# A hand-ordered FFT mixing kernel: output pair 0 in cosine and sine parts, and a re-ordered list of operations

## The chip, the cores and the metric

The kernel runs on one core of a Trainium2 chip. The core has five engines that work side by side: TensorE (PE in the profile, with weight loads as PEld), VectorE (DVE), ScalarE (ACT), GpSimd (POOL) and SyncE (SP), which here only issues transfers. Every engine takes its own instructions strictly in order and waits for the others by semaphores. The metric is the time of one launch in device microseconds (us), lower is better; the median of three runs of the kernel before is 114.5 us (114.27 to 114.72).

## What is computed

The input x is 2048 x 1024 (rows S, columns D, bfloat16). Two spectral filters A and B are applied to the same x, and a gate for each row mixes them:

```python
x = A_x
g = _sigmoid((x * gate_w).sum(-1, keepdims=True))
a = irfft2(rfft2(x) * (A_w_r + 1j * A_w_i)).astype(bfloat16)
b = irfft2(rfft2(x) * (B_w_r + 1j * B_w_i)).astype(bfloat16)
return g * a + (1 - g) * b
```

The two weights are 2048 x 513 complex each.

## The kernel before

The transforms are matrix products with small constant tables. The 2048 rows are split as 16 x 128 (s1, s2); the columns are folded by their symmetry into cosine and sine parts of even and odd frequencies. "Unit" n runs over 16 pieces of the spectrum: n = 0 to 7 hold the even column frequencies (par 0), n = 8 to 15 the odd ones (par 1). After the weights, the way back goes through a scratch tensor in device memory, which is written by unit and read by pair v: pair v holds output rows s1 = 2v and 2v+1, so there are 8 pairs of two rows (s = 0, 1), and each row has a first and a second half (h = 0, 1).

**The list.** The order of all work is written out by hand in the string ORDER (lines 24 to 65), some 570 tokens. A token names a function, its indices, then a PSUM bank (0 to 7) or an engine (A = ScalarE, D = VectorE, P = GpSimd, S = SyncE). Lines 856 to 858 call the functions in that order, and each engine runs its own tokens in the order of the list. Nothing reorders them later. So a token's place in the list decides what waits behind it on its engine, and a PSUM bank that is named again makes the later product wait until the earlier one has been read.

The stages, with their tokens and lines:

- **Forward along the rows.** x: (249) loads x in nine transfers. F1 (323 to 336) makes the even (e) or odd (o) part of one s1 on TensorE, 8 products of 128 columns. FC (411, copy on L201 or L203) moves half of it out of PSUM and FD (424, L422) folds both halves on VectorE, two operations of 256 elements; or FX (429) moves all of it and FP (435, also L422) folds on GpSimd. The result is the tile y. neg (275, L280) makes a negated table.
- **Forward along the columns, weights.** F2 (521, L528) and its copy T (532), F3 (549, L569) and its copy X (572), then the product with the weights P (577, L586), always on VectorE, 128 x 4096 elements. Y, NA and N (591 to 615) patch the two special columns of units 0 to 7: a small product on TensorE and two small operations on VectorE.
- **Back along the columns.** J (618, L632), 32 small products for each of the 16 units, needs P of its unit (and N, for units 0 to 7). R copies one half of it out of PSUM, on ScalarE (L201) or VectorE (L203). H (651, L654) stores that half to the scratch tensor and L:par:v (656, L665) loads pair v back, both on SyncE's queue: an L waits until all H of its par have landed.
- **The gate.** gc, GH, GC, Gt, GK, GZ, GS make sigmoid values from y; GA (L515) and GB (L519) make tables EA and EB of them on VectorE, four s1 at a time, with both inputs in SBUF. tab (299) runs a sigmoid once on ScalarE to load its table.
- **Back along the rows, and out.** V:par:v:s:bank (668, L675) applies EA and EB to one row of a pair, 8 products; VC (678) copies it to SBUF (two buffers). Then the last column transform: U (696, L703) makes a whole row in four products of 512 columns; C (705, L712) makes only the cosine part (256 columns) and the sine part (256 columns), in four products of 256. The two halves of the output row are cosine plus sine and cosine minus sine.

For par 0 the C result goes to EV, which holds the even part of a row: EX copies both parts to SBUF and EQ (803, L806) adds or subtracts them, on VectorE or GpSimd; or ES copies the sine part and EF (792, L796) does both sums on VectorE; or E (783) copies the two parts as they are, unsummed.

For par 1 the odd part is added to and subtracted from EV. Three ways are in use:

- OR (824, L826), two operations a row on VectorE, straight from a U in PSUM.
- OC (813) copies a U to SBUF and OP (819, L822) does the two operations on GpSimd.
- "Cosine and sine parts": EV was filled by E, unsummed, and the odd part is made by C. QD (828, L833) adds and subtracts par 1's parts to EV's parts on VectorE, two operations a row, into a float32 tile pq; then QP (835, L838) sums cosine and sine, four operations a pair (h, g), each over both rows, from pq in SBUF.

S:S:v (840, L847) stores a finished pair, in two halves for pair 7.

Of the kernel before, what the change touches and what calls it, by code (L numbers as in the profile page):

```python
# [29 lines left out]
FP:2:o FD:9:o FP:4:o F1:7:o:6 FX:6:o:A FD:8:e FD:9:e FC:10:e:A F1:13:e:5 c:S:PM FC:13:e:A F1:12:e:1 FC:12:e:A F1:5:o:4  # L30
FX:7:o:A F1:15:e:2 FC:15:e:A FD:11:e FD:10:e FD:12:e FD:13:e FX:5:o:A F1:13:o:7 F1:14:e:6 FP:6:o F1:15:o:0 FD:15:e FC:13:o:A
FP:7:o FP:5:o pw:P F1:12:o:4 FC:14:e:A F1:8:o:1 F1:10:o:5 FC:12:o:A FC:8:o:A FD:14:e FC:10:o:A neg:D:0:4 neg:D:4:16 FD:13:o
F2:1:1:2 F2:1:0:6 F2:0:0:3 FC:15:o:A T:1:1:A FD:10:o FD:8:o FD:12:o T:1:0:A W:S:2 W:S:6 T:0:0:A F1:14:o:7 F2:0:1:5 F1:11:o:6
T:0:1:A F3:1:2 FD:15:o FC:11:o:A F2:2:0:5 F2:2:1:4 FC:14:o:A X:1:A F3:0:0 FD:11:o T:2:0:A T:2:1:A X:0:A F2:4:1:6 F2:3:1:5
FD:14:o Y:1:4 T:3:1:A P:1:b F2:4:0:3 F2:3:0:2 Y:0:7 F3:2:0 GH:5 T:3:0:A T:4:0:A NA:1:D W:S:10 W:S:5 P:0:b W:S:3 W:S:7
c:S:WJ:4:16 F3:3:3 X:2:A W:S:9 NA:0:D T:4:1:A W:S:11 N:1:D W:S:4 GC:A J:1:6:0 F2:5:0:2 F2:5:1:5 P:2:b X:3:A R:1:1:A R:1:0:A
W:S:8 c:S:IG T:5:0:A Y:3:4 Y:2:1 Gt:0 F2:7:0:3 F3:4:6 T:5:1:A F2:7:1:2 X:4:A T:7:1:A N:0:D P:3:b GK:D NA:2:D NA:3:D N:2:D
J:0:0:4 N:3:D T:7:0:D R:0:1:A J:3:2:6 R:0:0:D GZ:0:0 F3:5:4 R:3:0:A R:3:1:D Y:4:6 GS:0 F2:6:0:7 X:5:A J:2:0:2 T:6:0:A P:4:b
NA:4:D R:2:0:D Y:5:4 R:2:1:A F2:6:1:7 GZ:1:5 T:6:1:A N:4:D GS:1 H:0:1 F3:7:1 H:1:0 H:3:0 H:0:0 H:1:1 X:7:A F2:8:1:5 T:8:1:A
# [872 lines left out]
```

## Time and profile before

| | |
|---|---|
| median of three runs | 114.5 us |
| the profiled execution's own time | 114.51 us |
| its span, first to last instruction | 112.7 us |
| mean granted TensorE clock | 0.987 |
| transfers | 36.79 MB, 326 GB/s over the span |
| HBM read, written | 23.96 MB, 12.58 MB |

The profile gives for each engine the time in which it was busy, the chain of work that ended last (followed back from the last instruction), groups of like instructions with their mean duration, and a timeline. Back-to-back operations of one engine overlap a little in the profile, so that eight operations of 0.68 us can take 4.87 us in a row: the step from one to the next (the pitch) is shorter than the duration. A number behind "x" is a count of instructions; in brackets or behind a bar stands the idle time before them, and what ended it.

### The profile page before, as it was taken

What the parts mean: (1) busy time and instruction counts of PE and PEld (TensorE: products, weight loads), DVE (VectorE), ACT (ScalarE), POOL (GpSimd) and SP (SyncE); (2) the same over time, 40 slices, a digit from 0 to 9 for tenths busy, and PEclk for the clock granted to TensorE, in tenths of its full rate; (3) what the DMA queues carried; (4) which work ended last, traced back from release to release, by engine and by line L of the source; (5) the groups of instructions that cost most, each with busy time, mean ns of one, the idle gap of its engine ahead of it and who ended that gap; (6) DMA issues with size and microseconds to landing.
All of it is one profiled execution on the core that took longest, in us unless ns stands there. A gap on an engine that the chain in (4) does not pass through costs nothing.

```text
span 112.7 us, 3824 instructions
## 1 busy us (share of the span) xinstructions
PE 99.4 (88%) x1556; PEld 69.8 (62%) x1559; DVE 100.1 (89%) x160; ACT 86.2 (76%) x141; POOL 43.0 (38%) x64
## 2 busy tenths in 40 slices
...
GB/s 70 368 309 398 405 379 400 398 260 413 410 412 412 372 298 326 394 298 186 237 302 292 420 407 307 385 377 325 295 246 398 337 385 329 196 192 186 372 372 186
DMA packets 17794, 36.79 MB, mean 326 GB/s; under 512 B 1904, under 2 KB 10736, under 8 KB 17776
## 3 DMA queue, kind: packets, MB, share of 16 engines
...
q8 instruction: 12, 0.20, 0.7%
...
HBM read 23.96 MB, written 12.58 MB: 324 GB/s over the span
## 4 chain that ended last, share of the span: by engine, by line
PE 32%; DVE 27%; DMA 16%; ACT 10%; issue 7%; SPq 4%; DVEq 1%; ACTq 0%
DVE p L586 9%; DVE y L422 9%; PE ps L703 8%; DMA ro<-sc 6%; DMA re<-in_x_dram 5%; DVE rl L203 5%; PE ps L632 5%; PE ps L528 5%; PE ps L675 5%; DMA sc<-rl 5%; ACT rl L201 4%; PE ps L569 4%; ACT T L201 3%; SPq L665 3%; PE ps L336 3%
## 5 line engine op out<-in xcount | busy, mean ns | idle before, releaser
L806 POOL TENSOR_TENSOR re<-wx 128x256 f32<-128x256 f32 x10 | 10.7, 1089 | 55.8 <-ACT wx L201 55.8
L201 ACT COPY wx<-ps 128x256 f32<-128x256 f32 (+1 forms) x41 | 18.3, 475 | 8.0 <-PE ps L336 4.5
L201 ACT CAST rl<-ps 128x1024 bf16<-128x1024 f32 x23 | 22.8, 1069 | 0.8 <-PE ps L632 0.6
L201 ACT CAST V<-ps 128x512 bf16<-128x512 f32 x26 | 14.9, 616 | 8.8 <-PE ps L675 4.4
L632 PE MATMUL ps<-p,wj 32*64 32x512 bf16 x512 | 18.2, 380 | 1.1 <-ACT rl L201 0.6
L528 PE MATMUL ps<-fd,y 128*128 128x256 bf16 x128 | 17.1, 273 | 1.3 <-ACT T L201 0.8
L586 DVE TENSOR_TENSOR p<-X,ro 128x4096 bf16<-128x4096 bf16 x8 | 18.2, 2278 | 0.0
L201 ACT CAST X<-ps 128x1024 bf16<-128x1024 f32 x16 | 17.3, 1079 | 0.1
L422 DVE TENSOR_TENSOR y<-ps,wx 128x256 bf16<-128x256 f32 x48 | 16.4, 414 | 0.5 <-ACT wx L201 0.5
L336 PE MATMUL ps<-f,re 128*128 128x128 bf16 x256 | 15.2, 219 | 1.6 <-DMA re<-in_x_dram 1.5
L336 PEld LDWEIGHTS <-re 128*128 128x128 bf16 x256 | 14.6, 98 | 2.4 <-DMA re<-in_x_dram 2.2
L201 ACT CAST T<-ps 128x512 bf16<-128x512 f32 x26 | 15.5, 647 | 0.5 <-PE ps L528 0.3
L528 PEld LDWEIGHTS <-y 128*128 128x128 bf16 x128 | 11.3, 97 | 5.9 <-issue 4.5
L632 PEld LDWEIGHTS <-wj 32*64 32x64 bf16 x512 | 8.3, 103 | 7.6 <-issue 4.1
L422 POOL TENSOR_TENSOR y<-wx 128x256 bf16<-128x256 f32 x16 | 11.3, 732 | 2.6 <-ACT wx L201 2.1
L826 DVE TENSOR_TENSOR ot<-re,ps 128x512 bf16<-128x512 f32 x18 | 11.3, 682 | 0.9 <-PE ps L703 0.4
L703 PE MATMUL ps<-ig,V 128*128 128x512 bf16 x45 | 11.2, 379 | 0.2
L712 PE MATMUL ps<-ig,V 128*128 128x256 bf16 x80 | 10.9, 273 | 0.2 <-ACT rl L201 0.2
L203 DVE CAST rl<-ps 128x1024 bf16<-128x1024 f32 x9 | 10.9, 1215 | 0.2 <-PE ps L632 0.2
L569 PE MATMUL ps<-T,wf 64*64 64x512 bf16 (+1 forms) x128 | 10.1, 333 | 1.1 <-DVE rl L203 0.4
L838 POOL TENSOR_TENSOR ot<-pq 128x512 bf16<-128x512 f32 x8 | 10.0, 1281 | 0.0
L675 PEld LDWEIGHTS <-re 128*128 128x128 bf16 x128 | 7.8, 98 | 2.4 <-issue 1.3
...
## 6 DMA issues: line engine op xcount, KB each, us to landing
sc<-rl SPq DMA_DIRECT2D x32, 256.0 KB, 4.1
...
```

The costliest lines, as they stand in the source:

```text
L201: nc.scalar.copy(out=out, in_=in_)
L203: Q[e].tensor_copy(out=out, in_=in_)
L336: nc.tensor.matmul(o, lhsT=lh, rhs=rh, start=(h == 0), stop=(h == 1))
L422: Q[e].tensor_tensor(yo[:, v, k:k + n, s1, :], a.rearrange("p (k c) -> p k c", c=4), b.rearrange("p (k c) -> p k c", c=4), op)
L528: nc.tensor.matmul(ps[:, v * 256:v * 256 + 256], lhsT=y[:, v, par, b, 2 * t:2 * t + 2, :, :].rearrange("p j s c -> p (j s c)"), rhs=C["FD" ...
L569: nc.tensor.matmul(view(ps[ho, tt * 512:(tt + 1) * 512], dst), lhsT=lh, rhs=view(T[hp(jh), tt, :], src), start=(w == 0), stop=(w == 1))
L586: nc.vector.tensor_tensor(p[:], xb, wb, ALU.mult)
L632: nc.tensor.matmul(o, lhsT=lh, rhs=src[r, ri, wi, tt], start=(q == 0), stop=(q == 3))
L675: nc.tensor.matmul(ps[:, ch * 128:ch * 128 + 128], lhsT=RR[par][:, v, ch // 2, s, c0 + 256 * ab:c0 + 256 * ab + 128], rhs=Ew[:, s1, :], st ...
L703: nc.tensor.matmul(ps, lhsT=Vs[par, v][:, s, ch, :], rhs=rh, start=(ch == 0), stop=(ch == 3))
L712: nc.tensor.matmul(ps[:, o:o + 256], lhsT=Vs[par, v][:, s, ch, :], rhs=g[:, o:o + 256], start=(ch % 2 == 0), stop=(ch % 2 == 1))
L826: nc.vector.tensor_tensor(otile(v)[:, s, h, :], EV[:, v, s], PS["O", 1, v, s], (ALU.add, ALU.subtract)[h])
```

## The change

Only the string ORDER changes; no function does. The list has 571 tokens in place of 572, and nearly all its lines differ, because tokens move by a few places and PSUM banks are renumbered.

**Pair 0.** Its even part is no longer summed: E:0:0 and E:0:1 on VectorE take the place of EX:0 (two, ScalarE) and of four EQ:0 (three on GpSimd, one on VectorE). Its odd part is made by C:1:0:0 and C:1:0:1 in place of two U; four QD:0 on VectorE and four QP:0 (three on GpSimd, QP:0:1:1 on VectorE) take the place of OC:0:0, two OP:0 (GpSimd) and two OR:0 (VectorE). Pairs 3 and 6 were already done in this way.

**Engines.** QP:3:1:1 and QP:6:1:0 move from GpSimd to VectorE. Of the EQ of pairs 1, 2 and 7, four move from VectorE to GpSimd and one (EQ:2:0:0) the other way. Of copies, VectorE gives up FX:1:o, one R and one T on balance, and takes some of VC, EX, ES and E in exchange for others. VectorE no longer has GB:12 close to the end of the weight products; it stands right after P:8.

**Order.** tab stands ahead of the first copy. The weight loads W and the constants are issued in another order. P keeps its order (1, 0, 2, 3, 4, 5, 7, 6, 8, 9, 10, 11, 12, 14, 13, 15). Behind the last scratch store, pairs of par 1 are loaded in the order 3, 1, 0, 5, 6, 7, 2, 4 (before 1, 3, 6, 7, 0, 2, 4, 5), and used by TensorE in the order 3, 1, 0, 6, 5, 2, 7, 4 (before 1, 3, 6, 0, 2, 5, 7, 4, by each pair's first V).

The start of the list, the lines around P:6 and P:8, and its end, before (-) and after (+):

```diff
-warm:8 c:A:F1 x:S:0:1 x:S:1:1 c:A:gws F1:0:o:4 x:S:2:2 F1:0:e:1 F1:1:e:6 F1:1:o:5 FC:0:e:A FC:1:e:A tab:A x:S:4:2 x:S:6:2
-c:S:E x:S:8:2 FX:0:o:D x:S:10:2 FD:0:e FD:1:e F1:2:e:7 F1:3:e:2 F1:3:o:0 FX:1:o:D FC:3:e:A F1:2:o:5 F1:5:e:4 x:S:12:2
...
-Y:7:0 F2:9:1:5 R:5:1:A F3:8:2 NA:7:D T:9:0:D F2:10:1:0 T:9:1:D F2:10:0:4 X:8:A T:10:1:A N:7:D GA:D:8 T:10:0:A F3:9:2 GA:D:4
-W:S:14 H:2:1 X:9:A J:7:6:0 N:6:D GA:D:0 P:8:b J:6:2:4 W:S:12 H:2:0 R:7:1:A H:3:1 R:6:0:D W:S:15 R:7:0:A H:5:0 H:5:1 GB:D:4
...
-V:0:2:0:2 VC:0:2:1:A VC:0:2:0:A EX:1:1:A H:12:0 J:14:0:4 J:13:6:2 R:14:0:A P:15:b H:11:1 R:14:1:A R:13:0:A C:0:2:1:1
-C:0:2:0:5 EX:2:0:A H:12:1 EX:2:1:D V:0:1:0:4 GB:D:12 R:13:1:D J:15:0:6 V:0:6:1:5 VC:0:1:0:A C:0:1:0:2 R:15:1:A V:0:6:0:4
-H:14:0 H:14:1 GB:D:8 R:15:0:D H:13:0 H:13:1 VC:0:6:1:A H:15:1 H:15:0 VC:0:6:0:A V:0:4:1:3 V:0:5:1:6 L:0:3 EX:1:0:A L:1:1
-L:1:3 L:1:6 EQ:0:0:1:D C:0:6:1:0 V:0:5:0:4 VC:0:5:1:D VC:0:5:0:D E:6:1:A EQ:2:1:0:D EQ:0:1:1:P L:1:7 L:1:0 L:1:2 L:1:4
-C:0:6:0:2 C:0:5:1:7 VC:0:4:1:A V:0:7:0:6 C:0:5:0:1 L:1:5 V:0:4:0:4 ES:5:1:A V:0:7:1:5 EQ:1:1:1:P VC:0:4:0:A E:6:0:D
-VC:0:7:0:D C:0:7:0:6 VC:0:7:1:A C:0:4:1:4 C:0:4:0:0 EX:7:0:A V:0:3:1:5 EQ:0:1:0:P EQ:2:0:1:P EQ:1:1:0:P EQ:2:0:0:P EQ:0:0:0:P
-EQ:2:1:1:P V:0:3:0:6 C:0:7:1:2 EQ:1:0:0:D VC:0:3:1:A VC:0:3:0:A EQ:1:0:1:D ES:5:0:D EF:5:1 EF:5:0 ES:4:1:D EF:4:1 C:0:3:1:5
-C:0:3:0:1 EX:7:1:A E:3:1:A E:3:0:A ES:4:0:A V:1:1:1:6 V:1:1:0:3 V:1:3:0:7 VC:1:1:0:A V:1:3:1:2 VC:1:3:0:A U:1:1:0:3
-VC:1:3:1:A EQ:7:0:0:D C:1:3:0:1 C:1:3:1:2 V:1:6:1:5 VC:1:1:1:D EF:4:0 EQ:7:1:1:D QD:3:0:0 OC:1:0:A QD:3:1:0 QD:3:1:1 QD:3:0:1
-U:1:1:1:3 EQ:7:0:1:P EQ:7:1:0:P OP:1:0:1 V:1:0:1:7 QP:3:0:1:P OP:1:0:0 QP:3:0:0:P VC:1:0:1:D VC:1:6:1:A C:1:6:1:5 V:1:0:0:6
-V:1:6:0:2 VC:1:0:0:A VC:1:6:0:A OR:1:1:1 U:1:0:1:7 QP:3:1:0:P U:1:0:0:1 QD:6:1:0 OR:1:1:0 OC:0:0:A V:1:2:1:4 VC:1:2:1:A
-OR:0:1:1 QD:6:1:1 QP:3:1:1:P C:1:6:0:0 V:1:2:0:2 V:1:5:1:5 V:1:5:0:4 OR:0:1:0 OP:0:0:1 QD:6:0:0 OP:0:0:0 QD:6:0:1 VC:1:2:0:D
-QP:6:1:0:P QP:6:0:1:P QP:6:1:1:P S:S:1 VC:1:5:1:A VC:1:5:0:A U:1:2:1:1 U:1:5:1:0 V:1:7:0:6 S:S:3 U:1:5:0:7 U:1:2:0:2
-V:1:7:1:5 V:1:4:0:4 VC:1:7:0:A V:1:4:1:3 OR:2:1:0 VC:1:7:1:A OR:2:1:1 OR:5:1:0 OR:5:1:1 OR:5:0:0 VC:1:4:0:A U:1:7:0:1
-OR:5:0:1 OR:2:0:0 S:S:0 QP:6:0:0:P VC:1:4:1:A U:1:4:0:4 S:S:5 OR:2:0:1 OR:7:0:1 OR:7:0:0 U:1:7:1:5 U:1:4:1:0 OC:4:0:A S:S:2
-OR:7:1:0 S:S:7:0 OR:7:1:1 S:S:6 OP:4:0:0 OP:4:0:1 OR:4:1:1 OR:4:1:0 S:S:7:1 S:S:4
+warm:8 c:A:F1 x:S:0:1 x:S:1:1 F1:0:o:0 F1:0:e:5 F1:1:e:3 F1:1:o:1 c:A:gws FX:0:o:D x:S:2:2 tab:A x:S:4:2 F1:2:e:2 x:S:6:2
+x:S:8:2 F1:3:e:6 FP:0:o gc:P FC:1:e:A c:S:E x:S:10:2 x:S:12:2 FX:1:o:A FC:0:e:A FD:1:e FC:2:e:A x:S:14:2 c:S:w0 FD:0:e
...
+R:5:0:A R:5:1:A T:9:0:A H:2:0 W:S:15 W:S:14 W:S:13 Y:7:4 T:9:1:D GA:D:4 F3:8:2 F2:10:1:1 F2:10:0:6 X:8:A T:10:0:A Y:6:0
+NA:7:D P:6:b H:4:0 H:4:1 NA:6:D F3:9:4 N:7:D N:6:D T:10:1:D J:7:6:0 P:8:b X:9:A R:7:1:A J:6:2:4 R:7:0:A GB:D:12 R:6:0:D
...
+R:12:1:A H:9:0 V:0:1:1:7 C:0:0:0:6 V:0:2:0:4 VC:0:1:1:A C:0:1:1:7 VC:0:2:1:A F3:15:2 VC:0:2:0:A R:12:0:D P:13:b EX:1:1:A
+J:14:0:4 H:10:1 H:9:1 X:15:A R:14:1:A H:10:0 H:11:0 H:12:1 E:0:0:D J:13:6:2 P:15:b R:14:0:A V:0:1:0:5 R:13:0:A H:12:0 H:11:1
+R:13:1:D C:0:2:1:4 J:15:0:6 VC:0:1:0:A EX:2:1:A R:15:0:A GB:D:8 R:15:1:D C:0:1:0:5 EX:1:0:A V:0:6:0:4 C:0:2:0:3 EQ:2:1:0:D
+V:0:6:1:1 VC:0:6:0:A V:0:5:1:0 H:14:1 V:0:5:0:5 EX:2:0:D H:14:0 H:13:1 H:13:0 C:0:6:0:7 VC:0:6:1:A VC:0:5:1:A H:15:0 E:6:0:A
+H:15:1 VC:0:5:0:A C:0:6:1:4 C:0:5:1:1 E:6:1:A L:0:3 EQ:2:0:0:D ES:5:1:D L:1:3 EQ:1:1:1:P EQ:1:1:0:P V:0:4:1:6 V:0:4:0:2
+V:0:7:1:5 C:0:5:0:3 EQ:2:1:1:P EQ:1:0:1:P VC:0:4:1:A EF:5:1 VC:0:4:0:D ES:5:0:D L:1:1 L:1:0 C:0:4:1:0 EQ:2:0:1:P EF:5:0
+C:0:4:0:7 V:0:7:0:6 VC:0:7:1:A C:0:7:1:4 V:0:3:1:5 VC:0:7:0:D V:0:3:0:1 C:0:7:0:3 ES:4:1:A ES:4:0:A EF:4:0 EX:7:1:D
+VC:0:3:1:A C:0:3:1:7 VC:0:3:0:A EX:7:0:A V:1:3:1:5 V:1:3:0:2 C:0:3:0:3 E:3:1:D L:1:5 L:1:6 L:1:7 L:1:2 VC:1:3:1:A VC:1:3:0:A
+EQ:1:0:0:P EQ:7:1:0:P C:1:3:1:7 EQ:7:0:1:P C:1:3:0:2 EF:4:1 E:3:0:A EQ:7:0:0:P QD:3:1:1 V:1:1:1:0 L:1:4 QD:3:0:1 VC:1:1:1:A
+V:1:1:0:1 V:1:0:0:6 U:1:1:1:0 VC:1:1:0:A VC:1:0:0:A V:1:0:1:3 C:1:0:0:6 QD:3:1:0 QD:3:0:0 U:1:1:0:5 VC:1:0:1:A V:1:6:1:2
+OC:1:0:A EQ:7:1:1:P QP:3:1:1:D C:1:0:1:3 VC:1:6:1:A OR:1:1:1 OR:1:1:0 V:1:5:0:1 V:1:6:0:5 V:1:5:1:2 QD:0:0:1 QD:0:0:0
+QD:0:1:1 C:1:6:1:6 QD:0:1:0 QP:0:1:1:D QD:6:1:0 QP:3:1:0:P QP:3:0:1:P QP:3:0:0:P VC:1:5:0:A VC:1:5:1:A VC:1:6:0:A S:S:3
+U:1:5:0:4 OP:1:0:1 V:1:2:1:1 C:1:6:0:7 U:1:5:1:2 V:1:2:0:3 QP:0:0:0:P QD:6:1:1 OP:1:0:0 V:1:7:0:5 VC:1:2:1:A U:1:2:1:6
+OR:5:0:1 V:1:7:1:0 QP:0:0:1:P VC:1:2:0:A OR:5:0:0 QP:0:1:0:P QD:6:0:0 S:S:1 VC:1:7:0:A U:1:2:0:1 OR:5:1:1 OR:5:1:0 QD:6:0:1
+OR:2:1:0 QP:6:0:0:P V:1:4:0:3 QP:6:1:1:P OR:2:1:1 VC:1:7:1:A VC:1:4:0:A U:1:7:0:0 V:1:4:1:2 S:S:5 S:S:0 U:1:4:0:6 U:1:7:1:5
+QP:6:0:1:P VC:1:4:1:A U:1:4:1:7 OR:2:0:0 OR:2:0:1 OR:7:0:1 OR:7:0:0 QP:6:1:0:D S:S:2 OR:7:1:1 S:S:7:0 OC:4:0:A OP:4:0:1 S:S:6
+OP:4:0:0 OR:7:1:0 S:S:7:1 OR:4:1:0 OR:4:1:1 S:S:4
```

More of the change, by code (lines that the diff above doesn't have):

```diff
@@ L30 @@
[L30 to L39, printed above, removed]
```

29 lines of the change are left out of this document (19 added, 10 removed).

## The prediction

> **What bounds the kernel now.** I read the page's busy shares first, then the stretches, the chain of waits, and the timelines of VectorE and GpSimd.
>
> ```profile
> span 112.7 us, 3824 instructions
> PE 99.4 (88%) x1556; PEld 69.8 (62%) x1559; DVE 100.1 (89%) x160; ACT 86.2 (76%) x141; POOL 43.0 (38%) x64
> 24.89:80.06 55.17, 50.50 (x964) 31.58 (x964) 54.90 (x59) 53.98 (x76) 8.14 (x7) 1.00 0.96 345
> 80.06:109.20 29.14, 26.84 (x284) 19.87 (x284) 26.12 (x50) 15.02 (x30) 19.84 (x18) 1.00 0.81 302
> 87.46:107.60 20.14, 19.44 (x191) 13.22 (x191) 17.43 (x31) 9.84 (x19) 16.59 (x14) 1.00 0.74 286
> ```
>
> Columns of the last three rows: the stretch, its length, then busy time of PE, PEld, DVE, ACT, POOL, the granted clock, transfers. From the first weight product (24.89) to the last scratch copy of VectorE (80.06), VectorE is busy 54.90 of 55.17 us and ScalarE 53.98. From 87.46 to 107.60 TensorE is busy 19.44 of 20.14. So there are two bounds in turn: VectorE, with ScalarE just beside it, and then TensorE, with VectorE close behind. A new wait on the bounding engine is paid in full, and only less work or fewer waits there can gain.
>
> ```profile
> 1.63 6.08 DMA re<-in_x_dram
> 10.61 8.88 DVE y L422 x26
> 79.00 1.15 DVE rl L203
> 80.16 2.38 DMA sc<-rl
> 85.72 7.16 DMA ro<-sc
> 92.92 0.62 PE ps L675 x8
> 96.60 0.45 PE ps L675 x8
> 97.05 0.44 PE ps L712 x4
> 104.06 3.47 PE ps L703 x16
> 107.56 0.41 DVE ot L826
> 108.57 0.60 DVE ot L826
> ```
>
> These pieces of the chain (start, length, what) show the joints: the third x transfer lands at 7.71; folds run from 10.61; the last copy R:15, its store, the loads of odd pairs; TensorE; two OR. They price TensorE: a V 0.45, a C 0.44, a U 3.47/4 = 0.87. VectorE ends at 109.17, and the last store takes the span to 112.7.
>
> **The front: 0 (from -0.6 to +0.5).**
>
> ```profile
> 20.25 4.71 DVE L422 TENSOR_TENSOR y<-ps,wx 128x256 bf16<-128x256 f32 x14
> 24.89 2.27 DVE L586 TENSOR_TENSOR p<-X,ro 128x4096 bf16<-128x4096 bf16 x1
> 6.22 1.28 ACT L301 ACT_TABLE_LOAD   x1
> L201 ACT COPY wx<-ps 128x512 f32<-128x512 f32 x16 | 10.0, 624 | 2.4 <-PE ps L703 2.3
> 10.29 0.33 SPq L254 DMA_DIRECT2D fd<-cst_fd  x1
> fd<-cst_fd SPq DMA_DIRECT2D x2, 256.0 KB, 6.2
> 19.71 1.47 PE L528 MATMUL ps<-fd,y 128*128 128x256 bf16 x12
> ```
>
> At 10.61 the 26 folds begin that run into the two negs and these 14, without a gap to 24.89. After the change the first five FD still wait for the third x transfer, which keeps its place in the queue, and FD:5 again starts near 10.6, with the same 40 folds and two negs behind it. The FX:1:o that VectorE gives up (about 0.6) is lost in that wait, as is the 1.28 us table load on ScalarE. Behind FC:14:e, X:1 now has one FX more ahead of it on ScalarE (0.5 in a row; that is the +0.5), but ScalarE, without the table load, is ahead by about as much there. The table FD:0:1 was issued at 10.29 and lands some 6.2 later, 16.5, for an F2 at 19.71; it is now queued behind WF:4:16 and PM, 0.5 MB more, which at the mean 326 GB/s is 1.6 us, and that fits.
>
> **The middle: the last R 0.5 earlier (from -0.8 to +1.0).**
>
> ```profile
> L203 DVE CAST rl<-ps 128x1024 bf16<-128x1024 f32 x9 | 10.9, 1215 | 0.2 <-PE ps L632 0.2
> L203 DVE CAST V<-ps 128x512 bf16<-128x512 f32 x6 | 4.1, 691 | 1.2 <-PE ps L675 1.1
> L203 DVE CAST T<-ps 128x512 bf16<-128x512 f32 x6 | 3.9, 681 | 0.0
> 54.07 0.41 DVE L519 TENSOR_TENSOR eb<-e,ea 128x512 bf16<-128x512 bf16 x1
> 76.37 0.94 DVE L519 TENSOR_TENSOR eb<-e,ea 128x512 bf16<-128x512 bf16 x1
> 74.07 2.27 POOL L806 TENSOR_TENSOR re<-wx 128x256 f32<-128x256 f32 x1 [3.26 <-ACT wx L201]
> L806 POOL TENSOR_TENSOR re<-wx x10: 719/731/2429, 68.4 to 87.5; 128x256 f32<-128x256 f32 x10
> 73.48 2.28 DVE L586 TENSOR_TENSOR p<-X,y 128x4096 bf16<-128x4096 bf16 x1
> ```
>
> In this stretch VectorE loses one T, one R and one EX (pitches of 0.60, 1.14, 0.61) and gains two VC and two E (four times 0.61): +0.1. ScalarE gains a T and an R and loses two VC and two EX: about -0.6, so it is no new bound. The other part is contention. The GB at 76.37 took 0.94, the one at 54.07 0.41; GpSimd was in an EQ in the first case and idle in the second. The other way round, the EQ that began at 74.07, inside P:15, took 2.27 where the median is 0.731. So an operation of either engine with both inputs in SBUF can hold the other up. After the change GB:12 stands behind P:8, with GpSimd idle: -0.5 (0 if GpSimd meets it anyway). One thing speaks against: J:7 needs N:7, now behind P:6, and a PSUM bank that T:10:0 frees behind a later X:8. It comes about 0.7 later and ScalarE slips with it; X:10 has more than that in hand before P:10, so 0 (0.7 if not). The last R then ends at 80.06 + 0.1 - 0.5 = 79.6.
>
> **The joint at J:15.** Behind P:15 (before: 73.48 to 75.76) VectorE now has only R:13:1, GB:8 and R:15:1, 1.14 + 0.4 + 1.14 = 2.7 us, where it had 4.3; E:0:0 stands ahead of P:15. So P:15 ends at 79.6 - 2.7 = 76.9, and
>
> ```profile
> 64.35 1.33 PE ps L632 x32
> 76.85 1.07 PE L632 MATMUL ps<-p,wj 32*64 32x512 bf16 x32
> 77.85 0.23 PE L675 MATMUL ps<-ea,re 128*128 128x128 bf16 x1
> ```
>
> J:15, 1.33 for its 32 products, ends near 78.3, where before TensorE had it done by 77.85: +0.4 on TensorE, but in time for R:15:1, which VectorE reaches at 78.4.
>
> **The tail on TensorE.** Between J:15 and the first odd V there was one C fewer (+0.44; 10 V and 12 C now). In the odd part two U become two C: 2 x 0.43 = -0.86. One wait goes:
>
> ```profile
> PE ps L675 <- DMA ro<-sc: 0.5, 1, 0.5
> ```
>
> V:1:0 waited 0.46 for L:1:0, queued fifth but used fourth; it is now third in both lists. (V:1:6, now behind the fifth load, is reached near 93.5, 0.6 after the fifth landed before.) Sum: 107.53 + 0.4 + 0.44 - 0.86 - 0.46 = 107.05.
>
> **The tail on VectorE and GpSimd.**
>
> ```profile
> 90.76 2.48 DVE L833 TENSOR_TENSOR pq<-re,ps 128x512 f32<-128x512 f32 x4 [0.90 <-PE ps L712]
> 99.78 4.87 DVE L826 TENSOR_TENSOR ot<-re,ps 128x512 bf16<-128x512 f32 x8
> L838 POOL TENSOR_TENSOR ot<-pq 128x512 bf16<-128x512 f32 x8 | 10.0, 1281 | 0.0
> L822 POOL TENSOR_TENSOR ot<-re,wx 128x512 bf16<-128x512 f32 x6 | 7.5, 1272 | 3.5 <-ACT wx L201 2.8 <-POOL ot L838 0.7
> 80.06 0.49 DVE L806 TENSOR_TENSOR re<-wx 128x256 f32<-128x256 f32 x1
> ```
>
> QD and OR step by 0.60 ((4.87 - 0.68)/7). From its first QD VectorE had 8 QD, 18 OR and 3 VC, 29 x 0.6 = 17.4 of the 18.4 us from 90.76 to 109.17. It will have 12 QD, 16 OR and 3 QP: 31. A QP on VectorE isn't in the trace; its 512 elements a partition are those of a QD, so 0.60; the bounds are 0.5 (the 256-element EQ at 80.06) and 1.28 (GpSimd's). Sum 18.6. But the first QD comes earlier: V:1:3 goes first and C:1:3:1 ends at 78.3 + 12 V (5.4) + 13 C (5.7) = 89.4, so QD starts at 89.6, and without waits VectorE ends at 108.3. GpSimd has 13 operations of 1.25 instead of 14; it is no bound by itself.
>
> The three QP on VectorE read two SBUF operands while GpSimd is nearly always in a QP or OP. If a QP comes while GpSimd holds the other up, it waits for the rest of 1.27. By their places in the list, QP:3:1:1 and QP:0:1:1 meet the end of a GpSimd operation and QP:6:1:0 its middle; I take 0.6 for the three together (from 0 to 3 x 1.27 = 3.8), and 0.1 for waits on TensorE. VectorE ends at 109.0, against 109.17.
>
> The Trainium skill has the same as a rule ("SBUF — State Buffer", "Who interferes with whom"): a VectorE instruction with two SBUF inputs contends with a GpSimd instruction that reads SBUF, and whichever issues first keeps the shared port for its whole length. By that rule the GB of 0.94 and the EQ of 2.27 are blocked instructions, and the trace agrees; it speaks against putting QP on VectorE here. By the rule the time is that of the blocked sums below, 115.6; by the EQ at 80.06 alone, which GpSimd hardly held up, it is 113.7.
>
> **Sum.** The span moves from 112.7 by 109.0 - 109.17 = -0.2 to 112.5. The profiled execution took 114.51, 1.8 more than its span, and the median is 114.5: forecast 114.3.
>
> **Rivals.**
>
> *The third pair pays in full.* The QP find GpSimd between operations, VectorE ends at 108.3 + 0.1 and TensorE keeps pace: 109.17 - 108.4 = 0.8 less, 113.7; with the front's 0.6 as well 113.1. For it: that VectorE waited for TensorE before (0.90 at 90.76), and that TensorE really has 0.86 less to do. Against: GpSimd is busy 16.59 of 20.14 us.
>
> *The sums shared with GpSimd block each other.* Place: the three QP on VectorE. Each waits for half a GpSimd operation on the mean, 3 x 0.64 = 1.9 in place of 0.6, and GpSimd loses three times 0.6, so that OP:4 ends late too: 114.3 + 1.3 = 115.6. It decides as soon as the three lose over 0.8 together. For it: the 0.94 and the 2.27. Against: the EQ at 80.06 took 0.49 with GpSimd busy, close to the 0.41 of an undisturbed one.
>
> *P:15 is late.* E:0:0 and two VC now stand ahead of P:15 on VectorE, and J:15, R:15, H:15 and all odd loads behind it. If GB:12's relief doesn't come, or VectorE waits 0.7 in the middle, P:15 ends by 77.9 and everything behind it moves by 0.7 to 1.0: 115.2.
>
> *The change doesn't do what it says:* TensorE's 0.86 is hidden, since VectorE carries two operations more and sets the end. That is half true in the forecast already; alone it gives 114.5.
>
> **How the numbers follow.** Within 0.5% of 114.5 is 113.9 to 115.1, about what a measurement can tell from no change. Forecast (114.3, own range 113.7 to 114.9) with the hidden gain 0.40: same 0.29, faster 0.07, slower 0.04. The third pair pays 0.26: faster. Blocked sums 0.20: slower. Late P:15 0.14: slower 0.12, same 0.02. So faster 0.33, same 0.31, slower 0.36. The range leaves out the blocked sums' upper half and the front's gain: 113.2 to 115.7.
>
> **What would show it.** VectorE's first weight product near 24.9; the last R near 79.6 and J:15 at 78.3; no wait for L:1:0; the first QD near 89.6; the three L838 on VectorE at 0.7 each (blocked: over 1); TensorE's last product near 107. I am wrong if VectorE waits more than 0.5 between 25 and 80, or if one QP lasts over 1.2.

## The result, and the profile after

The changed kernel took 113.97 us (median of 22 runs, 113.19 to 114.74), the kernel before 114.67 beside it (22 runs): a ratio of 0.9929, with an interval from 0.9903 to 0.9955. So it is 0.7% faster; ratios, here and below, leave disturbed runs out, so that they can differ from the quotient of the medians. Its profiled execution took 113.75 us, 0.76 less than that of before, and its span is 0.8 shorter. The head of its page, then its stretches (columns as in the prediction):

```profile
span 111.9 us, 3817 instructions
PE 97.9 (87%) x1559; PEld 69.9 (62%) x1559; DVE 99.3 (89%) x159; ACT 86.0 (77%) x141; POOL 40.7 (36%) x63
```

```profile
24.89:80.06 55.17, 48.89 (x954) 30.69 (x952) 54.99 (x61) 53.60 (x73) 3.73 (x4) 1.00 0.94 331
87.46:107.60 20.14, 19.17 (x199) 13.62 (x196) 19.52 (x34) 11.02 (x21) 19.25 (x17) 1.00 0.81 322
```

The first bound is as it was: VectorE is busy 54.99 of 55.17 us. In the tail the bound has moved from TensorE (19.44, now 19.17) to VectorE (17.43, now 19.52), and GpSimd has become nearly as full (16.59, now 19.25 of 20.14). TensorE isn't far from it: it works without a gap up to its end at 106.62.

**The front is late.** Timeline of VectorE, ScalarE's waits from 5 to 25 us, and timeline of GpSimd, of the changed kernel:

```profile
14.21 6.16 DVE L422 TENSOR_TENSOR y<-ps,wx 128x256 bf16<-128x256 f32 x18 [0.68 <-ACT wx L201]
...
25.28 2.27 DVE L586 TENSOR_TENSOR p<-X,ro 128x4096 bf16<-128x4096 bf16 x1
```

```profile
ACT wx L201 <- POOL y L422: 2.3, 2, 1.3
```

```profile
7.55 0.31 POOL L285 MEMSET gwz<- 128x256 bf16 x1
...
9.60 8.30 POOL L422 TENSOR_TENSOR y<-wx 128x256 bf16<-128x256 f32 x12
```

In the changed list gc:P stands behind FP:0:o. Its small operations hold GpSimd from 7.55 to 9.66; then GpSimd folds 12 times without a gap, ScalarE waits 2.3 us for GpSimd to give copy buffers back, and VectorE waits for ScalarE. The first weight product starts at 25.28, 0.39 later than in the trace of before.

**The middle and the joint.** Timelines of VectorE and of TensorE:

```profile
74.93 2.28 DVE L586 TENSOR_TENSOR p<-X,y 128x4096 bf16<-128x4096 bf16 x1
77.13 1.22 DVE L203 CAST rl<-ps 128x1024 bf16<-128x1024 f32 x1
78.26 0.41 DVE L519 TENSOR_TENSOR eb<-e,ea 128x512 bf16<-128x512 bf16 x1
78.60 1.22 DVE L203 CAST rl<-ps 128x1024 bf16<-128x1024 f32 x1
```

```profile
77.27 1.07 PE L632 MATMUL ps<-p,wj 32*64 32x512 bf16 x32
```

P:15 ends at 77.2, J:15 at 78.3, the last R at 79.8. From the first weight product to the last R's end it took 54.5 us, where before it took 55.2 (24.89 to 80.13).

**The tail.** VectorE's timeline, the group of QP on GpSimd (count, then min/median/max in ns), GpSimd's timeline, and the last U on TensorE:

```profile
89.54 2.48 DVE L833 TENSOR_TENSOR pq<-re,ps 128x512 f32<-128x512 f32 x4 [0.42 <-PE ps L712]
91.94 0.79 DVE L838 TENSOR_TENSOR ot<-pq 128x512 bf16<-128x512 f32 x1
...
96.24 0.68 DVE L838 TENSOR_TENSOR ot<-pq 128x512 bf16<-128x512 f32 x1
...
105.21 0.77 DVE L838 TENSOR_TENSOR ot<-pq 128x512 bf16<-128x512 f32 x1
105.90 2.47 DVE L826 TENSOR_TENSOR ot<-re,ps 128x512 bf16<-128x512 f32 x4
```

```profile
L838 POOL TENSOR_TENSOR ot<-pq x9: 1261/1272/1723, 90.9 to 104.2; 128x512 bf16<-128x512 f32 x9
```

```profile
90.91 4.19 POOL L838 TENSOR_TENSOR ot<-pq 128x512 bf16<-128x512 f32 x3 [0.47 <-DVE pq L833]
...
96.39 1.65 POOL L838 TENSOR_TENSOR ot<-pq 128x512 bf16<-128x512 f32 x1
...
105.60 2.73 POOL L822 TENSOR_TENSOR ot<-re,wx 128x512 bf16<-128x512 f32 x2 [0.17 <-ACT wx L201]
```

```profile
103.87 2.75 PE L703 MATMUL ps<-ig,V 128*128 128x512 bf16 x12
```

From 89.54 VectorE has no gap in 31 operations and ends at 108.37 (before 109.17). TensorE waits for no load and ends at 106.62 (before 107.53). The three QP on VectorE lost some 0.24 us together against 0.67 each, what a QD of the same size takes; GpSimd, beside the same three, lost more: about 0.43 in its first three QP (4.19, where one of 1.28 and two steps of 1.24 make 3.76), 0.38 in the one at 96.39, and 0.23 in its last two OP (2.73, undisturbed 2.50). GpSimd ends at 108.33, only 0.04 ahead of VectorE.

### The profile page after: what moved, and what is told of

Same layout as the page of the kernel before. It is cut to its first block, busy times and chain, and to the rows that moved or that the text cites. A ratio compares the mean times of both kernels' runs of the same rounds, so it can differ in the third digit from the quotient of the medians.

```text
span 111.9 us, 3817 instructions
## 1 busy us (share of the span) xinstructions
PE 97.9 (87%) x1559; PEld 69.9 (62%) x1559; DVE 99.3 (89%) x159; ACT 86.0 (77%) x141; POOL 40.7 (36%) x63
## 4 chain that ended last, share of the span: by engine, by line
DVE 31%; PE 30%; DMA 16%; issue 8%; POOL 6%; ACT 4%; SPq 1%; DVEq 1%; ACTq 0%; POOLq 0%
DVE p L586 13%; PE ps L675 10%; DMA sc<-rl 9%; DVE y L422 9%; PE ps L712 7%; DMA re<-sc 6%; PE ps L703 5%; POOL y L422 5%; PE ps L245 3%; DVE ot L826 3%; ACT rl L201 2%; PE ps L632 2%; DVE rl L203 1%; SPq L665 1%; ACT X L201 1%
## 5 line engine op out<-in xcount | busy, mean ns | idle before, releaser
L806 POOL TENSOR_TENSOR re<-wx 128x256 f32<-128x256 f32 x10 | 8.8, 900 | 60.6 <-ACT wx L201 53.5
L201 ACT CAST rl<-ps 128x1024 bf16<-128x1024 f32 x24 | 23.9, 1043 | 1.2 <-PE ps L632 0.7
L201 ACT COPY wx<-ps 128x256 f32<-128x256 f32 (+1 forms) x38 | 15.3, 458 | 7.9 <-PE ps L336 4.2
L336 PEld LDWEIGHTS <-re 128*128 128x128 bf16 x256 | 14.8, 99 | 2.0 <-issue 1.7
L838 POOL TENSOR_TENSOR ot<-pq 128x512 bf16<-128x512 f32 x9 | 12.0, 1361 | 0.5 <-DVE pq L833 0.5
L712 PE MATMUL ps<-ig,V 128*128 128x256 bf16 x88 | 12.2, 273 | 0.0
L826 DVE TENSOR_TENSOR ot<-re,ps 128x512 bf16<-128x512 f32 x16 | 9.9, 675 | 0.0
L703 PE MATMUL ps<-ig,V 128*128 128x512 bf16 x40 | 9.9, 379 | 0.0
L203 DVE CAST rl<-ps 128x1024 bf16<-128x1024 f32 x8 | 9.7, 1218 | 0.1
L586 DVE TENSOR_TENSOR p<-X,wx 128x4096 bf16<-128x4096 bf16 x4 | 9.1, 2283 | 0.0
```

The costliest lines, as they stand in the source:

```text
L201: nc.scalar.copy(out=out, in_=in_)
L203: Q[e].tensor_copy(out=out, in_=in_)
L336: nc.tensor.matmul(o, lhsT=lh, rhs=rh, start=(h == 0), stop=(h == 1))
L586: nc.vector.tensor_tensor(p[:], xb, wb, ALU.mult)
L703: nc.tensor.matmul(ps, lhsT=Vs[par, v][:, s, ch, :], rhs=rh, start=(ch == 0), stop=(ch == 3))
L712: nc.tensor.matmul(ps[:, o:o + 256], lhsT=Vs[par, v][:, s, ch, :], rhs=g[:, o:o + 256], start=(ch % 2 == 0), stop=(ch % 2 == 1))
```

## The experiments

Each is measured against the kernel before; a ratio is given with its interval. All but the three with another warm-up change the list ORDER alone.

**gc_first** (from the changed kernel): gc:P goes ahead of FP:0:o.

```diff
-F1:3:e:6 FP:0:o gc:P FC:1:e:A
+F1:3:e:6 gc:P FP:0:o FC:1:e:A
```

> The changed kernel with the gate's small preparation (gc) ahead of the first GpSimd fold (FP:0:o) again, as it stood before the change. Theory: in the changed kernel gc stands behind FP:0:o, so its nine small operations (7.55 to 9.66) push all later GpSimd folds about 2 us back, ScalarE waits twice for a temporary that GpSimd still reads (2.3 us in all) and VectorE starts its weight products at 25.28 instead of 24.89. Then with gc first GpSimd's folds start about 2 us earlier, ScalarE's two waits are gone, the first product starts at 24.6 to 24.9 and the time falls by 0.3 to 0.6 us against the changed kernel: ratio to before 0.988 to 0.991. Rival: the late start is that of the first TensorE products (4.57 instead of 4.29) and of the x transfers: first product still at 25.2 to 25.4, ratio 0.993.

Measured: 113.54 us, 0.989 (0.984 to 0.994). ScalarE's waits for GpSimd were gone, the first weight product began at 24.19, and the last R ended at 78.7, 1.1 earlier than in the changed kernel. But the first QD began only at 89.35. SyncE's queue (two stores to each of the first two rows, then the first odd load), then TensorE's waits from 83 to 95:

```profile
77.28 1.86 SPq L654 DMA_DIRECT2D sc<-rl  x2
79.24 0.96 SPq L654 DMA_DIRECT2D sc<-rl  x2
83.14 0.33 SPq L665 DMA_DIRECT2D ro<-sc  x1
```

```profile
PE ps L675 <- DMA ro<-sc: 0.7, 1, 0.7
```

The four last scratch stores went out from 77.28 to 80.2, and the odd loads only at 83.14, 0.45 earlier than in the changed kernel; TensorE, which had waited for none there, now waits for them. So the front's gain reached the joint between scratch stores and loads, and most of it stayed there. Four profiled executions with gc:P behind FP:0:o (the changed kernel and the three experiments on pair 0 and on QP that are made from it) began the weight products at 25.28, 24.86, 25.54 and 25.52, the four with gc:P first (three of them below) at 24.19, 24.75, 24.89 and 24.86: on the mean 0.6 apart. The kernel before and the four experiments made from it, all with one and the same front, lie between 24.28 and 24.89, so single traces differ by as much, and only the groups can be compared. One more, after_warm53, whose warm-up is 0.6 shorter (3.01 us in place of 3.60), began at 24.52 with gc:P behind. The times are 0.4% apart in the medians, and their intervals overlap.

**qp_gpsimd** (from the changed kernel): the three QP on VectorE back to GpSimd, in their places.

```diff
-EQ:7:1:1:P QP:3:1:1:D C:1:0:1:3
+EQ:7:1:1:P QP:3:1:1:P C:1:0:1:3
-QD:0:1:0 QP:0:1:1:D QD:6:1:0 QP:3:1:0:P
+QD:0:1:0 QP:0:1:1:P QD:6:1:0 QP:3:1:0:P
-OR:7:0:0 QP:6:1:0:D S:S:2
+OR:7:0:0 QP:6:1:0:P S:S:2
```

> The changed kernel with its three QP of VectorE (QP:3:1:1, QP:0:1:1, QP:6:1:0) back on GpSimd. Theory: sharing the sums pays, since GpSimd would have 16 operations of 1.25 from 90.9 on, 20.0 us, and end near 111, where it ends at 108.3 with 13; VectorE has 28 instead of 31 and waits. Time +1.5 to +2.5 us against the changed kernel, ratio to before 1.006 to 1.015. Rival: on VectorE the three lose as much by blocking as they save: ratio 0.990 to 0.996.

Measured: 119.35 us, 1.042 (1.036 to 1.047). GpSimd's and VectorE's timelines show that this ran into something else:

```profile
95.38 4.97 POOL L838 TENSOR_TENSOR ot<-pq 128x512 bf16<-128x512 f32 x4 [3.62 <-DVE pq L833]
```

```profile
106.83 3.68 DVE L826 TENSOR_TENSOR ot<-re,ps 128x512 bf16<-128x512 f32 x6 [3.25 <-DMA out_dram<-ot]
```

QP:0:1:1, on GpSimd now, stands ahead of the QP of pair 3 and waits 3.62 us for its QD; everything behind it is late, the output buffers come free late, and VectorE waits 3.25 for one. It priced a bad order, not the sharing.

**qp_gpsimd2** (from the changed kernel): the same, with QP:3:1:1 put just ahead of QP:3:1:0 and QP:0:1:1 just behind QP:0:1:0, so that each is ready when GpSimd comes to it.

> Again the changed kernel with all QP on GpSimd, now each in the place where its operands are ready first (QP:3:1:1 ahead of QP:3:1:0, QP:0:1:1 behind QP:0:1:0). In the earlier run GpSimd stood 3.6 us behind QP:0:1:1, which waited for QD:0. Theory: GpSimd's 16 operations of 1.25 run from 90.5 almost without a gap and end at 110.5 to 112, ratio to before 1.010 to 1.025. Rival: that order was not what cost: GpSimd ends near 113.8 again, ratio 1.04.

Measured: 116.17 us, 1.014 (1.009 to 1.018). GpSimd's timeline at the end:

```profile
99.75 8.67 POOL L838 TENSOR_TENSOR ot<-pq 128x512 bf16<-128x512 f32 x7
108.36 2.50 POOL L822 TENSOR_TENSOR ot<-re,wx 128x512 bf16<-128x512 f32 x2
```

No QP is held up (1.24 us a step), and GpSimd ends at 110.86, behind VectorE (108.7). Against 0.9929, the sharing is worth 2.1%, some 2.4 us: with a third pair in parts, GpSimd alone would be the bound.

**pair0_rows** (from the changed kernel): pair 0 as before the change, in the new order of the rest (its EX stay on VectorE, where the changed list has E); the diff in part.

```diff
-E:0:1:D
+EX:0:1:D
...
-C:1:0:0:6
+U:1:0:0:6
...
-QD:0:0:1 QD:0:0:0 QD:0:1:1
+OR:0:1:1
...
-QP:0:0:0:P
+OP:0:0:1
```

> The changed kernel with pair 0 as it was before the change (EX and four EQ, two U, OR and OP), in the changed order, so only two pairs are in cosine and sine parts. Theory: the third pair is worth TensorE's 0.86 us: TensorE, which now ends at 106.6 without a wait in the tail, ends near 107.5, VectorE has 3 operations fewer (28) and waits for it, and ends near 109.0 instead of 108.4. Time +0.4 to +0.8 us against the changed kernel, ratio to before 0.996 to 1.000. Rival: the gain is the order of the tail (odd pairs 3, 1, 0 first, the earlier first QD), not the pair: ratio 0.990 to 0.994, VectorE's end at or below 108.4.

Measured: 115.1 us, 1.004 (1.000 to 1.007). VectorE's timeline:

```profile
96.28 1.29 DVE L826 TENSOR_TENSOR ot<-re,ps 128x512 bf16<-128x512 f32 x2 [1.79 <-PE ps L703]
98.13 1.29 DVE L833 TENSOR_TENSOR pq<-re,ps 128x512 f32<-128x512 f32 x2 [0.56 <-PE ps L712]
```

TensorE is the bound again, VectorE waits 2.35 us for it here, and ends at 109.7. The third pair in parts is worth 1.1% (1.0036 less 0.9929), 1.2 us; the new order without it is no faster than the kernel before. Not all of that is TensorE's 0.86. With pair 0's EQ back on GpSimd, VectorE is held up in the middle too, a weight product takes 2.59 us in place of 2.28, and the stretch from the first product to the last R takes 54.9 in place of 54.5:

```profile
72.39 2.59 DVE L586 TENSOR_TENSOR p<-X,y 128x4096 bf16<-128x4096 bf16 x1
```

**pair0_alone** (from the kernel before): the third pair in parts (E on ScalarE, where EX was) and the same three QP on VectorE, all else in the old order, PSUM banks too.

```diff
-U:1:0:1:7
+C:1:0:1:7
...
-OR:0:1:0 OP:0:0:1 QD:6:0:0 OP:0:0:0
+QD:0:1:0 QD:0:0:1 QD:0:0:0 QP:0:1:1:D QD:6:0:0
...
-QP:6:1:0:P QP:6:0:1:P
+QP:0:0:0:P QP:0:0:1:P QP:0:1:0:P QP:6:0:1:P
```

> The kernel before with one part of the change: pair 0 in cosine and sine parts (E in place of EX and EQ, C in place of U, QD and QP in place of OR and OP), with the same three QP on VectorE, and everything else in the old order. Theory: the pair is worth 0.86 us of TensorE in any order; TensorE's end moves from 107.5 to 106.7 and VectorE, with two operations more behind its first QD (which stays near 90.8), ends at 108.4 to 108.9. Ratio to before 0.993 to 0.998. Rival: the pair needs the new order of the tail, because the first QD must come earlier (89.5 instead of 90.8) to make room for the two operations: then VectorE ends at 109.2 or later, ratio 1.000 to 1.010.

Measured: 116.73 us, 1.018 (1.013 to 1.023). TensorE's waits from 84 us on, and VectorE's end:

```profile
PE ps L703 <- DVE pq L833: 2.2, 2, 1.4
```

```profile
108.41 2.47 DVE L826 TENSOR_TENSOR ot<-re,ps 128x512 bf16<-128x512 f32 x4
```

VectorE's first QD came at 90.44, 0.9 later than in the changed kernel, two VC still stood between its sums, and TensorE waited 2.2 us for VectorE to free its banks. So neither half gains without the other, as tried: the edit loses 1.8% in the old order, the new order gains nothing without the edit. Only one placing of the new tokens was tried in the old order; other places or banks might wait less.

The same trace shows what helps VectorE in the middle. Its GB, GB:12 in its old place among them:

```profile
76.23 0.41 DVE L519 TENSOR_TENSOR eb<-e,ea 128x512 bf16<-128x512 bf16 x1
...
77.70 0.48 DVE L519 TENSOR_TENSOR eb<-e,ea 128x512 bf16<-128x512 bf16 x1
```

In the kernel before, these two took 0.94 and 0.64. The four EQ of pair 0, three of them on GpSimd, are gone, and from the first product to the last R it took 54.6 us, nearly all that the changed kernel gains there.

**gb12_early** (from the kernel before): GA:12 and GB:12 directly behind P:8.

```diff
+P:8:b GA:D:12 GB:D:12 J:6:2:4
-P:8:b J:6:2:4
```

> The kernel before with one thing of the change: GA:12 and GB:12 stand behind P:8, where GpSimd is idle, instead of among the last weight products. Theory: the GB that took 0.94 there takes 0.41, the last R copy on VectorE ends about 0.5 us earlier (79.6 instead of 80.1), the odd loads start as much earlier, and the wait of TensorE for L:1:0 (0.46) shrinks: 0.2 to 0.5 us, ratio 0.996 to 0.998. Rival: TensorE sets the end and does not start earlier, so the copy ends earlier but the time stays: ratio 0.999 to 1.001.

Measured: 116.64 us, 1.019 (1.013 to 1.025). The contention went as expected (all four GB 0.42 to 0.43, the last R 0.4 earlier, though half of that is a first product that began 0.2 earlier), but two VectorE operations now stood ahead of R:6:0, so the stores of units 6 and 7 landed late and the even loads began at 60.51 (before 58.34). Stretches of this kernel, last column but one the transfers' share:

```profile
60.00:62.00 2.00, 1.59 (x44) 1.19 (x51) 2.00 (x3) 1.71 (x3) 0.00 (x0) 1.00 0.37 51
...
72.00:80.00 8.00, 7.49 (x147) 4.87 (x145) 7.66 (x7) 7.66 (x12) 4.62 (x5) 1.00 1.09 380
80.00:84.00 4.00, 4.00 (x61) 3.82 (x58) 2.75 (x6) 2.62 (x6) 2.03 (x3) 1.00 1.04 339
```

From 60 to 62 the queues are idle for over a microsecond (before: 0.94 busy), and from 64 to 84 full, as they nearly are in the kernel before (1.03, 0.99 and 0.96 in the same stretches): what was not moved in that microsecond isn't made up. The last scratch store, issued at 80.17 (80.16 in the kernel before), took 4.4 us to land (before: 2.4), and the odd loads began at 84.79 (before 82.74). The transfers are a third bound, and the little won on VectorE can't be seen behind it.

**gb12_mid** (from the kernel before): the same two behind GB:0, after P:10, where no even store waits.

> The kernel before with GA:12 and GB:12 moved behind GB:0 (after P:10) instead of behind P:8. In the earlier run they stood ahead of R:6:0, whose store H:6:0 is among the last that the loads L:0 wait for: the loads began at 60.5 instead of 58.3 and the odd loads at 84.8 instead of 82.7. Theory: that store was the cost, and the relief of the GB (0.94 to 0.41) is real but small: L:0:0 near 58.3 again, ratio to before 0.996 to 1.001. Rival: any GA and GB ahead of the later products costs, as everything behind them is late by 0.8: ratio 1.005 to 1.02.

Measured: 115.15 us, 1.003 (1.000 to 1.007). The even loads began at 57.65 and the odd ones at 82.78, so the cost of gb12_early is gone: it was R:6:0. The relief by itself is worth nothing that can be measured: of the four GB one still took 0.82, and from the first product to the last R it took 55.1 us (before 55.2).

**l10_first** (from the kernel before): L:1:0 ahead of L:1:7.

```diff
-L:1:7 L:1:0 L:1:2
+L:1:0 L:1:7 L:1:2
```

> The kernel before with one part of the change: the load L:1:0 goes ahead of L:1:7, so that it is fourth in the queue as it is in use. Theory: TensorE's wait of 0.46 us at 92.9 is gone and the end moves by it: ratio to before 0.996 to 0.998. Rival: the wait is passed on, since the loads behind it are late too or VectorE holds the PSUM banks: ratio 0.999 to 1.002, with a wait of TensorE or none at another place.

Measured: 114.28 us, 0.996 (0.993 to 0.999), as priced. TensorE's wait of 0.46 was gone, but one of 0.28 for a copy by ScalarE (VC) came in its place, at 92.59:

```profile
PE ps L712 <- ACT V L201: 0.3, 1, 0.3
```

So the trace shows only part of the price. VectorE's end came 0.78 earlier (108.39), but 0.61 of that is there at the first weight product (24.28), where the two lists are the same; from the first QD to the end it took 18.23 us in place of 18.41. Theory and rival are both half right, and where the rest of the 0.4% comes from is open.

**gc_warm53, gc_warm30 and after_warm53.** These asked why the four last stores went out so slowly in gc_first: the issue of one lasted 1.41 us, where most last 0.36 to 0.45. A packet of 16 KB on queue q8, which carries instruction code, had begun 0.4 us earlier. All three change the warm-up's products (their result is unused), to shift TensorE's code: in gc_warm53 from gc_first,

```diff
-            nc.tensor.matmul(ps[:, 0:512], lhsT=warm[:, 0:128], rhs=warm, start=True, stop=True)
+            nc.tensor.matmul(ps[:, 0:64], lhsT=warm[:, 0:128], rhs=warm[:, 0:64], start=True, stop=True)
-warm:8
+warm:53
```

> The kernel with gc:P ahead of FP:0:o, and in its warm-up 53 products of 64 columns in place of 8 of 512 (their result is never used). About the same warm-up time, but 45 products and 45 weight loads, 90 instructions, more on TensorE ahead of everything. In the kernel without this, the issue of the store H:13:0 on SyncE's queue lasted 1.41 us (77.73 to 79.14) where others last 0.36 to 0.45, and H:15:1, whose rows were ready at 78.72, was issued only at 79.75. A 16 KB packet of instruction code on queue q8 began at 77.3. Theory A: the code packet slows the issue, and its place is tied to TensorE's instruction count (172 PE and PEld instructions in the 3.7 us before it). Then 90 instructions more move it 1.9 us earlier, to about 75.4 to 76.4, where SyncE issues nothing (75.4 to 77.28): all four last stores are issued in 0.36 to 0.5, H:15:1 at 78.8, odd loads from 82.2 (before 83.14), first QD near 88.5, span near 110.9, time 112.6, ratio 0.982 (0.978 to 0.986). Theory B: the long issue has another cause (stores in flight, the row it reads), and the packet only coincides: H:13:0 again over 0.9, odd loads at 83.1, ratio 0.989 as without it. Theory C: the store-to-load joint isn't what held the tail: odd loads come earlier, but the first QD stays near 89.3 and the ratio near 0.989.

gc_warm30 is made in the same way, with 128 columns and warm:30.

> As the last, with 30 products of 128 columns in the warm-up: 22 products and 22 weight loads, 44 instructions, more than with 8 products of 512. Theory A (code packet, tied to TensorE's instruction count): it moves by half as much, 0.95 us, to about 76.3 to 77.3, just ahead of H:13:1 at 77.28: the issues of H:13:0 and H:15 last 0.5 or less, H:13:1's perhaps up to 0.9; H:15:1 issued at 78.8 to 79.3, odd loads 82.2 to 82.7, ratio 0.981 to 0.987. Theory B (another cause): H:13:0 over 0.9 again, ratio 0.989.

after_warm53 is the changed kernel with the warm-up of gc_warm53.

> The changed kernel as it is, with the warm-up of 53 products of 64 columns alone. There the packet on q8 began at 79.0, the issue of H:15:0 lasted 0.96 (79.41 to 80.37), and H:15:1 was issued at 80.47 with its rows ready at 79.82. Theory A: the packet comes 1.5 to 1.9 us earlier, 77.1 to 77.5, and is over at the first of the last stores (78.37): H:15:1 issued at 79.9, odd loads 83.0 (before 83.59), up to 0.5 less time: ratio 0.986 to 0.992 against the kernel before (0.9929 without). Theory B: H:15:0 over 0.9 again, odd loads 83.6, ratio 0.993.

Measured: 114.78 us, 0.999 (0.996 to 1.003); 113.38 us, 0.988 (0.984 to 0.992); 115.06 us, 0.998 (0.994 to 1.002). In gc_warm53 the packet came at 76.9 and the four last stores were issued in 0.44 to 0.48 each, H:15:1 at 79.47 with its rows ready at 79.29: so far theory A (the first weight product began 0.56 later than in gc_first, which moves A's times to 79.4 and, for the odd loads, 82.8). But the odd loads began at 83.40 all the same, 3.9 us behind it. And another packet met those loads; the transfers of gc_warm53 from 84.6 to 84.7 (queue, kind: packets, MB, share), then its SyncE queue:

```profile
q8 instruction: 1, 0.02, 141.1%
```

```profile
84.73 2.50 SPq L665 DMA_DIRECT2D ro<-sc  x1
```

The issue of the fourth odd load lasted 2.50 us, and in after_warm53 that of the third 1.55. TensorE waited 1.8 us in gc_warm53, for the first odd load, which had gone out before, at 83.40, and took 5.7 us to land (3.4 to 4.3 in the other six of the seven traces that the last section counts); the first QD came at 91.12. That the packet or the long issue made that load late isn't shown. In gc_warm30 the packet came at 78.5, not at 76.3, H:15:0's issue lasted 0.94, and nothing was won on gc_first. So theory A is right that the long issues here met a code packet, wrong on where the packet comes (it moved by less than the instructions added, or not at all), and wrong that the issues set the odd loads. What set them is the landing of the last store: in all fourteen traces the first odd load goes out 0.2 us behind it (gc_first 82.94 and 83.14, gc_warm53 83.20 and 83.40, before 82.54 and 82.74). In gc_warm53 the last four stores went out 0.5 to 0.6 apart but landed about 0.7 apart, each behind the one before, so their earlier issue won nothing there. B came near with its odd loads at 83.1, for another reason than B's; C's earlier odd loads didn't come at all.

**gc_l03** (from gc_first) tried what else could hold them: L:0:3, 0.5 MB, moves from behind the last scratch store to ahead of the last four.

```diff
-H:14:0 H:13:1
+H:14:0 L:0:3 H:13:1
-E:6:1:A L:0:3 EQ:2:0:0:D
+E:6:1:A EQ:2:0:0:D
```

> The kernel with gc:P ahead of FP:0:o, and the load L:0:3 (0.5 MB, even pair 3, needed near 85) moved from behind the last scratch store to behind H:14:0, so that it goes out near 75.4 in place of 80.25. Without this move the transfers were busy 0.35, 0.76 and 0.35 of the three us from 77 to 80, and then 1.0, while the last two stores and L:0:3 were under way together; H:15:1 took 3.39 from its issue to the first odd load. Theory A: the last stores share the queues with L:0:3; ahead of them it fills the idle 1.5 us (0.55 MB). Then odd loads begin 2.6 us (as in the kernel before) behind H:15:1, 82.3 in place of 83.14, TensorE's waits of 1.0 and 0.7 for them go, first QD at 88.5 (89.35), VectorE ends at 107.4 (108.2), span 111.0, ratio 0.981 (0.978 to 0.986). Theory B: a store's way to landing is what it is, whatever is beside it, or L:0:3 only holds up the stores behind it: odd loads at 83.1 or later, ratio 0.989 to 0.995. Theory C: odd loads at 82.3, but the first QD no earlier than 89.1, as TensorE's even products take that long: ratio 0.987.

Measured: 113.98 us, 0.988 (0.982 to 0.994). Its stretches:

```profile
81.00:82.00 1.00, 1.00 (x13) 0.91 (x11) 0.00 (x0) 0.83 (x2) 1.00 (x2) 1.00 1.09 382
82.00:83.00 1.00, 1.00 (x22) 1.00 (x19) 0.86 (x3) 1.00 (x3) 0.06 (x1) 1.00 0.42 146
83.00:84.00 1.00, 1.00 (x15) 0.89 (x12) 1.00 (x3) 0.35 (x2) 0.00 (x0) 1.00 0.03 9
84.00:85.00 1.00, 1.00 (x15) 0.95 (x14) 0.97 (x3) 1.00 (x3) 0.00 (x0) 1.00 0.40 41
```

The queues stayed full up to about 82.4 and then stood idle, with a share of 0.03 from 83 to 84, until the last store had landed and the odd loads, issued at 83.83, had begun to move. Theory B: ahead of the stores L:0:3 lands first (80.92), the four stores behind it 0.7 apart up to 83.63, and the odd loads follow. In its old place it fills the time in which a store's landing is waited for. By how much the move holds them up isn't shown: the first weight product began at 24.86 here, 0.67 later than in gc_first, and from the last R to the odd loads both took 4.4 us (gc_warm30, with L:0:3 in its old place, 3.7). The time shows no loss either, 0.988 against 0.989.

## Why the prediction was right, point by point

The forecast was 114.3, and the measured 113.97 lies in its own range; the ratio, 0.7% faster, is a little beyond the half per cent that the forecast kept within, and 0.9929 of the 114.5 it started from is 113.7, the lower edge of that range. The span came out 0.6 below the forecast (111.9 against 112.5). Over half of that is one term, the three QP (0.24 lost where 0.6 was put); another 0.1 was set aside for waits on TensorE that didn't come.

- *Front, 0:* wrong, +0.39, inside its range. The step read the wait for the third x transfer as setting the start of the folds, and left out that gc:P, moved behind FP:0:o, holds GpSimd and with it ScalarE's copies. In gc_first ScalarE's waits for GpSimd were gone. The middle made up for it, so that it didn't reach J:15; that the two errors met is luck.
- *Middle, 0.5 earlier:* the durations were right, the reason only in part. All GB took 0.41 to 0.42, as priced, and from the first weight product to the last R it took 0.7 less than before (54.5 against 55.2), where the prediction's 24.9 and 79.6 make some 0.5 less. Contention between VectorE and GpSimd was the right place to look, but moving GB:12 is neither enough to end it nor needed. Alone in the old order the move shortened the stretch by 0.1 (gb12_mid). With GB:12 in its old place but pair 0's EQ gone it was shorter by 0.7 (pair0_alone), and with the EQ back in the new order it lost 0.4 again (pair0_rows). The prediction's middle doesn't count the EQ that go. GA:12 and GB:12 together behind P:8 lost 1.9% in the old order (gb12_early), by a mechanism that the prediction missed: R:6:0 late, stores late, transfers late. In the changed kernel GB:12 alone stands in front of R:6:0.
- *Joint at J:15:* right: P:15 ended at 77.2 (76.9 forecast), J:15 at 78.3 (78.3). The end agrees so well because J:15 took 1.07 in place of 1.33, which made up for the later P:15.
- *TensorE's tail:* the terms were right, the sum 0.4 too high: the last product ended at 106.62 against 107.05. By the prediction's own prices the 26 V, 18 C and 10 U behind J:15 take 28.3 us, and they took 28.3. The 26 V, 15 C and 12 U of before take 28.7 by the same prices, but took 29.7; of that 0.9 of waiting the sum took off only the 0.46 for L:1:0. VectorE, which had no gap, set the end.
- *First QD at 89.6:* right, 89.54, although the odd loads came 0.85 later than before, which the prediction hadn't seen.
- *The three QP lose 0.6:* this is the term that was mis-sized. They lost 0.24, and VectorE ended at 108.37, where the rival "the third pair pays in full" put it at 108.4. The place of QP:6:1:0 was wrong: it began 0.22 us before the end of a GpSimd operation, not in the middle of one. GpSimd paid about 1.0 in their place, hidden behind VectorE's end with 0.04 to spare.
- *Rivals.* The third pair pays in full: its numbers came out, VectorE's end at 108.37 and a profiled execution of 113.75 against 108.4 and 113.7, and the pair is worth 1.2 us between pair0_rows and the changed kernel. Its condition did not: the QP met GpSimd inside an operation each time, and what they cost fell on GpSimd, which had just that much room. Blocked sums: not on VectorE; on GpSimd about 1.0 of the 1.8 that this rival puts there. Late P:15: its place was there, but P:15 ended at 77.2, short of the 77.9 from which it decides. A hidden gain of TensorE: no, as pair0_rows waited 2.35 us for it.

By the rule of the Trainium skill ("SBUF — State Buffer", "Who interferes with whom") the one that issues second blocks until the first is done. The trace agrees with it, if each operation is set against what was left of the other when it began. The three QP on VectorE began 0.24, 0.09 and 0.22 us before the end of the GpSimd operation then running, and lost 0.12, 0.01 and 0.10. On GpSimd it was the operations that began while a QP of VectorE ran that grew, the one at 96.39 and these two:

```profile
92.13 1.72 POOL L838 TENSOR_TENSOR ot<-pq 128x512 bf16<-128x512 f32 x1
105.60 1.51 POOL L822 TENSOR_TENSOR ot<-re,wx 128x512 bf16<-128x512 f32 x1 [0.17 <-ACT wx L201]
```

In order of time, the three had 0.59, 0.53 and 0.38 us of the QP ahead of them and lost 0.45, 0.38 and 0.24. So on either engine the second operation lost what was left of the first, less 0.1 to 0.15 us. The prediction drew 115.6 from the rule by letting each QP meet half a GpSimd operation; at the places where they really met, the same rule gives no more than 0.55 on VectorE.
